# GroupNorm over 134 MB: weights of the identity loaded once a tile, and loops without a remainder

## The chip, the cores and the metric

The kernel runs on one core of one Trainium2 chip. The metric is the device time of one execution in microseconds (us), given as the median of several runs. A profiled execution gives a trace beside it: for each engine, what ran when, and for the DMA engines their packets and landings. Times inside the trace count from the start of its span.

## The reference

The input x has 128 images of 1024 channels of 32 x 16 values in bf16. The channels form 32 groups of 32. Each group of each image is normalised by its own mean and variance, and each channel then gets a scale and an offset:

```python
xr = x.reshape(B, G, C // G, H, W)
mu = xr.mean(axis=(2, 3, 4), keepdims=True)
var = ((xr - mu) ** 2).mean(axis=(2, 3, 4), keepdims=True)
xn = (xr - mu) / jnp.sqrt(var + 1e-5)
xn = xn.reshape(B, C, H, W)
return xn * g[None, :, None, None] + b[None, :, None, None]
```

So 134 MB are read and 134 MB are written, and each value is needed twice: for the statistics and for the result.

## The kernel before

One tile is four images: 128 partitions (4 images x 32 groups), each with the 16,384 values of one group, 32 KB a partition and 4 MB in all. There are NT = 32 tiles and SLOTS = 6 buffers x0 to x5 in SBUF; tile i uses buffer i % 6. Every buffer has its own small tiles (nshift, sq, negmean and so on) and its own semaphores.

All loads and stores are issued by SyncE (SP), in an order written out by hand: the six first loads, with the two small ones for g and b behind the first; then for each tile i its store, followed by the load of tile i + 5. A store waits until VectorE is done with the tile (s_done); a load waits until the store that empties its buffer has landed (s_store). At the end SyncE waits for the last store of every buffer.

Three engines work on a tile, each in its own loop:

- TensorE (`sums`, L181): 32 matmuls of an identity matrix (`eye`) with 512 columns of the tile each, accumulated in one PSUM bank ps. This adds up the 32 parts of each partition. Every matmul call issues two instructions: LDWEIGHTS, which loads the identity into the array, and MATMUL.
- ScalarE (`squares`, L194): the mean of the first 512 values as a shift (L197), then four passes over a quarter of the tile each that sum the squares of the shifted values (L208); after VectorE's variance the square root (L217).
- VectorE (`normalise`, L221): the sum of ps gives the mean (L224); with ScalarE's squares the variance (L235 to L248), the reciprocal of the root, scale and offset per channel (L258 to L264); then 32 instructions that write the result over the tile in place, one for each channel of the group (L274).

The loops are real loops on the engines, with a counter in a register. One iteration holds the code of six tiles, one for each buffer; the counter gives the values that the semaphores are waited for. As 32 is not a multiple of 6, there are ROUNDS = 5 iterations, and behind them the code of REST = 2 more tiles:

```python
with act.Fori(1, ROUNDS + 1) as n:
    n16 = act.snap(n * 16)
    for j in range(SLOTS):
        squares(j, n16, n)
for j in range(REST):
    squares(j, 16 * (ROUNDS + 1), ROUNDS + 1)
```

[...]

Of the kernel before, what the change touches and what calls it, by code (L numbers as in the profile page):

```python
# [16 lines left out]
SLOTS = 6  # L17
MM_FREE = 512
# [4 lines left out]
def kernel(  # L23
# [13 lines left out]
    nc = tc.nc  # L37
# [6 lines left out]
    NT = B0 // NS  # L44
    F = KC * HW
    inv_n = 1.0 / float(F)
    NMM = F // MM_FREE
    SQ = F // SQ_PARTS

    x_v = x.rearrange("(t n) (q k) h w -> t (n q) (k h w)", n=NS, q=G)  # L50
    o_v = out.rearrange("(t n) (q k) h w -> t (n q) (k h w)", n=NS, q=G)
# [5 lines left out]
    def sb(name, shape, dtype):  # L57
        return ctx.enter_context(nc.sbuf_tensor(name, shape, dtype))

    def sem(name):  # L60
        return tc.alloc_semaphore(name)

    xs = [sb(f"x{j}", [P, F], BF16) for j in range(SLOTS)]
    ps = [
        ctx.enter_context(nc.psum_tensor(f"ps{j}", [P, MM_FREE], F32))
        for j in range(SLOTS)
    ]
# [9 lines left out]
    eye = sb("eye", [P, P], BF16)  # L77
    ja = sb("ja", [P, HW], BF16)
    js = sb("js", [P, SQ], BF16)
    jd = sb("jd", [P, MM_FREE], BF16)  # L80
# [16 lines left out]
    def sems(name):  # L97
        return [sem(f"{name}{j}") for j in range(SLOTS)]

    s_load = sems("load")  # L100
    s_store = sems("store")
# [19 lines left out]
    sp, pe, act, dve, pool = nc.sync, nc.tensor, nc.scalar, nc.vector, nc.gpsimd  # L121

    def load(i):
        j, n = i % SLOTS, i // SLOTS
        if n > 0:
            sp.wait_ge(s_store[j], 16 * n)
        sp.dma_start(out=xs[j][:], in_=x_v[i]).then_inc(s_load[j], 16)  # L127

    def store(i):
        j, n = i % SLOTS, i // SLOTS  # L130
        sp.wait_ge(s_done[j], n + 1)
        sp.dma_start(out=o_v[i], in_=xs[j][:]).then_inc(s_store[j], 16)

# [2 lines left out]


    load(0)
    sp.dma_start(out=gam_b[:], in_=four(g_v)).then_inc(s_gb, 16)
    sp.dma_start(out=bet_b[:], in_=four(b_v)).then_inc(s_gb, 16)  # L140
    for i in range(1, SLOTS):
        load(i)
    for i in range(NT):
        store(i)
        if i >= 1 and i + SLOTS - 1 < NT:
            load(i + SLOTS - 1)
    for j in range(SLOTS):
        sp.wait_ge(s_store[j], 16 * len(range(j, NT, SLOTS)))


    dve.memset(eps_t[:], EPS).then_inc(s_eps, 1)  # L151
# [3 lines left out]
        out=half[:],  # L155
# [9 lines left out]
        out=eye[:],  # L165
# [12 lines left out]
    dve.wait_ge(s_gbf, 1)  # L178
    pe.wait_ge(s_eye, 1)

    def sums(j, n16):  # L181

        pe.wait_ge(s_load[j], n16)
        for k in range(NMM):
            m = pe.matmul(  # L185
                out=ps[j][:],
                lhsT=eye[:],
                rhs=xs[j][:, k * MM_FREE : (k + 1) * MM_FREE],
                start=(k == 0),
                stop=(k == NMM - 1),  # L190
            )
        m.then_inc(s_sum[j], 1)

    def squares(j, n16, n):  # L194

        act.wait_ge(s_load[j], n16)
        act.activation(  # L197
            out=ja[:],
            in_=xs[j][:, 0:HW],
            func=ACT.Identity,  # L200
            scale=-1.0 / HW,
            accum_out=nshift[j][:],
        ).then_inc(s_shift[j], 1)
        act.wait_ge(s_shift[j], n)
        for k in range(SQ_PARTS):
            if k > 0:
                act.wait_ge(s_part[k - 1][j], n)
            act.activation(  # L208
                out=js[:],
                in_=xs[j][:, k * SQ : (k + 1) * SQ],  # L210
                func=ACT.Square,
                bias=nshift[j][:],
                scale=1.0,
                accum_out=sq[j][:, k : k + 1],
            ).then_inc(s_part[k][j], 1)
        act.wait_ge(s_var[j], n)
        act.activation(  # L217
            out=std[j][:], in_=var[j][:], func=ACT.Sqrt, bias=eps_t[:], scale=1.0
        ).then_inc(s_std[j], 1)

    def normalise(j, n):  # L221

        dve.wait_ge(s_sum[j], n)
        dve.tensor_scalar(  # L224
            out=jd[:],
            in0=ps[j][:],
            scalar1=-inv_n,
            scalar2=None,
            op0=ALU.mult,
            op1=ALU.add,  # L230
            accum_out=negmean[j][:],
        ).then_inc(s_mean[j], 1)
        dve.wait_ge(s_mean[j], n)
        dve.wait_ge(s_part[SQ_PARTS - 1][j], n)  # L234
        dve.tensor_tensor(  # L235
            out=d[j][:], in0=negmean[j][:], in1=nshift[j][:], op=ALU.subtract
        ).then_inc(s_d[j], 1)
        dve.wait_ge(s_d[j], n)
        dve.tensor_scalar(  # L239
            out=nd2[j][:],  # L240
            in0=d[j][:],
            scalar1=d[j][:],
            scalar2=-1.0,
            op0=ALU.mult,
            op1=ALU.mult,
        ).then_inc(s_nd2[j], 1)
        dve.wait_ge(s_nd2[j], n)
        dve.tensor_scalar(  # L248
            out=jv[:],
            in0=sq[j][:],  # L250
            scalar1=inv_n,
            scalar2=nd2[j][:],
            op0=ALU.mult,
            op1=ALU.add,
            accum_out=var[j][:],
        ).then_inc(s_var[j], 1)
        dve.wait_ge(s_std[j], n)
        dve.reciprocal(out=rstd[j][:], in_=std[j][:]).then_inc(s_rstd[j], 1)  # L258
        dve.wait_ge(s_rstd[j], n)
        dve.tensor_scalar(  # L260
            out=scl[j][:], in0=gam[:], scalar1=rstd[j][:], scalar2=None, op0=ALU.mult
        ).then_inc(s_scl[j], 1)
        dve.wait_ge(s_scl[j], n)
        dve.scalar_tensor_tensor(  # L264
            out=bia[j][:],
            in0=scl[j][:],
            scalar=negmean[j][:],
            in1=bet[:],
            op0=ALU.mult,
            op1=ALU.add,  # L270
        ).then_inc(s_bia[j], 1)
        dve.wait_ge(s_bia[j], n)
        for k in range(KC):
            v = dve.tensor_scalar(  # L274
                out=xs[j][:, k * HW : (k + 1) * HW],
                in0=xs[j][:, k * HW : (k + 1) * HW],
                scalar1=scl[j][:, k : k + 1],
                scalar2=bia[j][:, k : k + 1],
                op0=ALU.mult,
                op1=ALU.add,  # L280
            )
        v.then_inc(s_done[j], 1)


    ROUNDS = NT // SLOTS
    REST = NT % SLOTS
    with pe.Fori(16, 16 * ROUNDS + 1, 16) as n16:
        for j in range(SLOTS):
            sums(j, n16)
    for j in range(REST):  # L290
        sums(j, 16 * (ROUNDS + 1))

    with act.Fori(1, ROUNDS + 1) as n:
        n16 = act.snap(n * 16)
        for j in range(SLOTS):
            squares(j, n16, n)
    for j in range(REST):
        squares(j, 16 * (ROUNDS + 1), ROUNDS + 1)

    with dve.Fori(1, ROUNDS + 1) as n:  # L300
        for j in range(SLOTS):
            normalise(j, n)
    for j in range(REST):
        normalise(j, ROUNDS + 1)


# [28 lines left out]
```

## Time and profile before

| | |
|---|---|
| median of 3 runs | 634.16 us (633.76 to 634.39) |
| the profiled execution | 634.32 us |
| its span | 632.6 us, so 1.72 us lie outside |
| bytes moved | 268.53 MB, mean 424 GB/s |
| ScalarE, VectorE busy | 519.3 us (82%), 395.0 us (62%) |
| TensorE: matmuls, weight loads | 286.1 us (45%), 112.7 us (18%) |
| one tile on ScalarE (four passes of L208) | 4 x 3,708 ns |
| weight load, median | 98 ns, 1,024 of them |
| load and store, median from issue to landing | 29.2 us, 38.4 us |

The profile's page gives busy times by engine, the span in 40 slices, the DMA queues and the chain of work that ended last. In the views of stretches each row has the stretch, its length, the busy time of PE (matmuls), PEld (weight loads), VectorE, ScalarE and GpSimd with the number of instructions, the TensorE clock granted, the busy share of the 16 DMA engines, and GB/s. A row of the chain has start, duration and what ran. In the waits a row has who waited for whom, the sum in us, how many times, and the longest.

### The profile page before, as it was taken

How to read it: one execution, taken by the hardware profiler on the slowest of the kernel's cores; microseconds unless marked ns; L12 is line 12 of the kernel's file. 1: busy time of each engine (PE TensorE's matmuls, PEld its weight loads, DVE VectorE, ACT ScalarE, POOL GpSimd, SP SyncE). 2: the span in 40 equal slices, each digit the busy share in tenths (PEclk: the TensorE clock that was granted, in tenths of full speed). 3: DMA queues.
4: the chain of work that ended last, by engine and by line, in shares of the span. 5: the costliest groups of instructions: out<-in, count | busy, mean ns of one | idle time of the engine just before them, and what ended most of it. 6: DMA issues, size and time to landing. Idle time of an engine off the chain costs nothing.

```text
span 632.6 us, 3913 instructions
## 1 busy us (share of the span) xinstructions
PE 286.1 (45%) x1007; PEld 112.7 (18%) x1024; DVE 395.0 (62%) x1316; ACT 519.3 (82%) x354; POOL 0.8 (0%) x6
## 2 busy tenths in 40 slices
PE   1977404553245632456433655334553335643300
PEld 0332101221112211122111222111221112221100
DVE  0177777766666667777655676555775556765550
ACT  2999999999999999997878978789888889887700
POOL 0000000000000000000000000000000000000000
PEclk9988858766787667876678776678765787666755
DMA  9999999999999999999999999999999999999994
GB/s 366 431 430 417 434 433 431 433 429 427 435 431 429 433 431 433 437 433 433 435 431 433 429 431 431 431 435 433 431 433 433 437 431 437 433 430 431 433 431 204
DMA packets 9487, 268.53 MB, mean 424 GB/s; under 512 B 1288, under 2 KB 1288, under 8 KB 1288
## 3 DMA queue, kind: packets, MB, share of 16 engines
q1 hardware_dynamic: 9480, 268.46, 98.7%
q8 instruction: 2, 0.03, 0.0%
q14 instruction: 5, 0.04, 0.0%
HBM read 134.23 MB, written 134.22 MB: 424 GB/s over the span
## 4 chain that ended last, share of the span: by engine, by line
DMA 73%; ACT 18%; DVE 4%; SPq 1%; issue 0%; DVEq 0%
DMA out_dram<-x 67%; ACT js L208 17%; DMA x<-in_x_dram 7%; DVE x L274 3%; ACT ja L197 1%; SPq L127 1%; ACT std L217 0%; DVE jv L248 0%; DVE nd L239 0%; DVE d L235 0%; DVE bia L264 0%; DVE scl L260 0%; DVE rstd L258 0%; DVEq L234 0%; DVEq L300 0%
## 5 line engine op out<-in xcount | busy, mean ns | idle before, releaser
L208 ACT ACTIVATE js<-x,nshift 128x4096 bf16<-128x4096 bf16 x128 | 474.7, 3708 | 4.1
L185 PE MATMUL ps<-x,eye 128*128 128x512 bf16 x1007 | 286.1, 451 | 304.3 <-DMA x<-in_x_dram 302.5
L274 DVE TENSOR_SCALAR x<-x,scl,bia 128x512 bf16<-128x512 bf16 x1024 | 333.7, 422 | 1.2
L185 PEld LDWEIGHTS ps<-x,eye 128*128 128x128 bf16 x1024 | 112.7, 113 | 477.2 <-DMA x<-in_x_dram 317.8
L235 DVE TENSOR_TENSOR d<-negmean,nshift 128x1 f32<-128x1 f32 x32 | 5.1, 160 | 167.3 <-ACT js L208 167.3
L197 ACT ACTIVATE ja<-x 128x512 bf16<-128x512 bf16 x32 | 19.9, 623 | 47.9 <-DMA x<-in_x_dram 47.7
L224 DVE TENSOR_SCALAR_CACHE_REDUCE jd<-ps 128x512 bf16<-128x512 f32 x32 | 22.5, 703 | 16.4 <-PE ps L185 16.2
L217 ACT ACTIVATE std<-var,eps_t 128x1 f32<-128x1 f32 x32 | 9.4, 294 | 25.8 <-DVE jv L248 25.8
L208 ACT ACTIVATION_READ_ACCUMULATOR js<-x,nshift 128x1 f32 x128 | 23.9, 186 | 0.0
L258 DVE RECIPROCAL rstd<-std 128x1 f32<-128x1 f32 x32 | 5.2, 164 | 11.6 <-ACT std L217 11.6
L264 DVE SCALAR_TENSOR_TENSOR bia<-scl,negmean,bet 128x32 f32<-128x32 f32 x32 | 8.1, 252 | 1.1
L260 DVE TENSOR_SCALAR scl<-gam,rstd 128x32 f32<-128x32 f32 x32 | 7.7, 242 | 1.1
L176 DVE CAST gam<-gam_b 128x32 f32<-128x32 bf16 x1 | 0.2, 181 | 12.4 <-DMA bet_b<-in_b_dram 12.4
L248 DVE TENSOR_SCALAR_CACHE_REDUCE jv<-sq,nd 128x4 f32<-128x4 f32 x32 | 7.0, 218 | 1.1
L239 DVE TENSOR_SCALAR nd<-d 128x1 f32<-128x1 f32 x32 | 6.8, 214 | 1.1
L197 ACT ACTIVATION_READ_ACCUMULATOR ja<-x 128x1 f32 x32 | 6.0, 186 | 0.0
L224 DVE DVE_READ_ACCUMULATOR jd<-ps 128x1 f32 x32 | 3.2, 99 | 0.0
L248 DVE DVE_READ_ACCUMULATOR jv<-sq,nd 128x1 f32 x32 | 2.7, 84 | 0.0
L174 ACT ACT_TABLE_LOAD x1 | 1.3, 1283 | 1.0 <-SPq L55 1.0
L151 DVE MEMSET eps_t<- 128x1 f32 x1 | 0.1, 59 | 1.1 <-SPq L55 1.1
L154 POOL TENSOR_SCALAR_AFFINE_SELECT half<-ones 128x128 bf16<-128x128 bf16 x1 | 0.3, 292 | 0.9 <-DVE ones L152 0.9
L164 POOL TENSOR_SCALAR_AFFINE_SELECT eye<-half 128x128 bf16<-128x128 bf16 x1 | 0.3, 292 | 0.1
(7 smaller groups left out, 0.9 us busy)
## 6 DMA issues: line engine op xcount, KB each, us to landing
x<-in_x_dram SPq DMA_DIRECT2D x32, 4096.0 KB, 29.2
out_dram<-x SPq DMA_DIRECT2D x32, 4096.0 KB, 38.4
gam_b<-in_g_dram SPq DMA_DIRECT2D x1, 8.0 KB
bet_b<-in_b_dram SPq DMA_DIRECT2D x1, 8.0 KB
```

The costliest lines, as they stand in the source:

```text
L127: sp.dma_start(out=xs[j][:], in_=x_v[i]).then_inc(s_load[j], 16)
L185: m = pe.matmul(out=ps[j][:], lhsT=eye[:], rhs=xs[j][:, k * MM_FREE : (k + 1) * MM_FREE], start=(k == 0), stop=(k == NMM - 1),)
L197: act.activation(out=ja[:], in_=xs[j][:, 0:HW], func=ACT.Identity, scale=-1.0 / HW, accum_out=nshift[j][:],).then_inc(s_shift[j], 1)
L208: act.activation(out=js[:], in_=xs[j][:, k * SQ : (k + 1) * SQ], func=ACT.Square, bias=nshift[j][:], scale=1.0, accum_out=sq[j][:, k : k + 1],
L217: act.activation(out=std[j][:], in_=var[j][:], func=ACT.Sqrt, bias=eps_t[:], scale=1.0).then_inc(s_std[j], 1)
L224: dve.tensor_scalar(out=jd[:], in0=ps[j][:], scalar1=-inv_n, scalar2=None, op0=ALU.mult, op1=ALU.add, accum_out=negmean[j][:],).then_inc(s ...
L239: dve.tensor_scalar(out=nd2[j][:], in0=d[j][:], scalar1=d[j][:], scalar2=-1.0, op0=ALU.mult, op1=ALU.mult,).then_inc(s_nd2[j], 1)
L248: dve.tensor_scalar(out=jv[:], in0=sq[j][:], scalar1=inv_n, scalar2=nd2[j][:], op0=ALU.mult, op1=ALU.add, accum_out=var[j][:],).then_inc(s ...
L258: dve.reciprocal(out=rstd[j][:], in_=std[j][:]).then_inc(s_rstd[j], 1)
L260: dve.tensor_scalar(out=scl[j][:], in0=gam[:], scalar1=rstd[j][:], scalar2=None, op0=ALU.mult).then_inc(s_scl[j], 1)
L264: dve.scalar_tensor_tensor(out=bia[j][:], in0=scl[j][:], scalar=negmean[j][:], in1=bet[:], op0=ALU.mult, op1=ALU.add,).then_inc(s_bia[j], 1)
L274: v = dve.tensor_scalar(out=xs[j][:, k * HW : (k + 1) * HW], in0=xs[j][:, k * HW : (k + 1) * HW], scalar1=scl[j][:, k : k + 1], scalar2=bi ...
```

## The change

In `sums` only the first matmul of a tile loads the identity. The other 31 are written as bare MATMUL instructions that use the weights already in the array (`again`).

The loops have six iterations and no code behind them. Six iterations of six buffers would be 36 tiles, so in the first iteration the four buffers 0 to 3 are skipped by a branch (`If`). Tile i therefore uses buffer (i + 4) % 6: tiles 0 and 1 use buffers 4 and 5, tile 2 buffer 0, and so on. In the later iterations buffers 0 to 3 wait for counts that are lower by one than those of buffers 4 and 5, hence the second set of registers (m, m16).

```diff
+    FIRST = -NT % SLOTS
+    ROUNDS = (NT + FIRST) // SLOTS
...
     def load(i):
-        j, n = i % SLOTS, i // SLOTS
+        j, n = (i + FIRST) % SLOTS, i // SLOTS
...
     def store(i):
-        j, n = i % SLOTS, i // SLOTS
+        j, n = (i + FIRST) % SLOTS, i // SLOTS
...
     for j in range(SLOTS):
-        sp.wait_ge(s_store[j], 16 * len(range(j, NT, SLOTS)))
+        sp.wait_ge(s_store[j], 16 * len(range((j - FIRST) % SLOTS, NT, SLOTS)))
...
+    def again(first, rhs, stop):
+
+        return pe.add_instruction(
+            mybir.InstMatmult(
+                name=nc.get_next_instruction_name(),
+                ins=[pe.lower_ap(rhs), first.ins[1]],
+                outs=[first.outs[0]],
+                start_tensor_calc=False,
+                stop_tensor_calc=stop,
+                tile_size=first.tile_size,
+                tile_position=first.tile_position,
+                ldweights=False,
+            )
+        )
+
     def sums(j, n16):
 
         pe.wait_ge(s_load[j], n16)
-        for k in range(NMM):
-            m = pe.matmul(
-                out=ps[j][:],
-                lhsT=eye[:],
-                rhs=xs[j][:, k * MM_FREE : (k + 1) * MM_FREE],
-                start=(k == 0),
-                stop=(k == NMM - 1),
-            )
+        m = pe.matmul(out=ps[j][:], lhsT=eye[:], rhs=xs[j][:, 0:MM_FREE], start=True, stop=False)
+        for k in range(1, NMM):
+            m = again(m.ins, xs[j][:, k * MM_FREE : (k + 1) * MM_FREE], k == NMM - 1)
         m.then_inc(s_sum[j], 1)
...
-    ROUNDS = NT // SLOTS
-    REST = NT % SLOTS
...
     with act.Fori(1, ROUNDS + 1) as n:
         n16 = act.snap(n * 16)
-        for j in range(SLOTS):
+        m, m16 = act.snap(n - 1), act.snap(n16 - 16)
+        with act.If(n > 1):
+            for j in range(FIRST):
+                squares(j, m16, m)
+        for j in range(FIRST, SLOTS):
             squares(j, n16, n)
-    for j in range(REST):
-        squares(j, 16 * (ROUNDS + 1), ROUNDS + 1)
```

The loops of TensorE and VectorE are changed in the same way.

More of the change, by code (lines that the diff above doesn't have):

```diff
@@ L282, in normalise @@
         v.then_inc(s_done[j], 1)
-    ROUNDS = NT // SLOTS
-    REST = NT % SLOTS
     with pe.Fori(16, 16 * ROUNDS + 1, 16) as n16:
-        for j in range(SLOTS):
+        m16 = pe.snap(n16 - 16)
+        with pe.If(n16 > 16):
+            for j in range(FIRST):
+                sums(j, m16)
+        for j in range(FIRST, SLOTS):
             sums(j, n16)
-    for j in range(REST):
-        sums(j, 16 * (ROUNDS + 1))
     with act.Fori(1, ROUNDS + 1) as n:
         n16 = act.snap(n * 16)
-        for j in range(SLOTS):
+        m, m16 = act.snap(n - 1), act.snap(n16 - 16)
+        with act.If(n > 1):
+            for j in range(FIRST):
+                squares(j, m16, m)
+        for j in range(FIRST, SLOTS):
             squares(j, n16, n)
-    for j in range(REST):
-        squares(j, 16 * (ROUNDS + 1), ROUNDS + 1)
     with dve.Fori(1, ROUNDS + 1) as n:
-        for j in range(SLOTS):
+        m = dve.snap(n - 1)
+        with dve.If(n > 1):
+            for j in range(FIRST):
+                normalise(j, m)
+        for j in range(FIRST, SLOTS):
             normalise(j, n)
-    for j in range(REST):
-        normalise(j, ROUNDS + 1)
 _INS = ['x', 'g', 'b']
```

## The prediction

> **What bounds the kernel now.** I read the page's totals first, then the DMA queues, then the chain of work that ended last, then what SyncE's queue waited for, and last the stretches after the final load.
>
> ```profile
> PE 286.1 (45%) x1007; PEld 112.7 (18%) x1024; DVE 395.0 (62%) x1316; ACT 519.3 (82%) x354; POOL 0.8 (0%) x6
> ...
> DMA  9999999999999999999999999999999999999994
> ...
> q1 hardware_dynamic: 9480, 268.46, 98.7%
> q8 instruction: 2, 0.03, 0.0%
> q14 instruction: 5, 0.04, 0.0%
> ```
>
> No compute engine is full; the 16 DMA engines are, in every slice but the last. The two "instruction" queues are loads of the engines' own code, by the same DMA engines. They are seven packets, but they matter below.
>
> ```profile
> 551.84 29.14 DMA x<-in_x_dram
> ...
> 581.00 0.73 ACT ja L197 x2
> ...
> 598.96 10.43 DVE x L274 x32
> ```
>
> From the end of the chain of waits: the last load lands at 580.98, ScalarE and VectorE work on that tile until 609.4, and then its store goes out. It lands at 630.0. So is this chain of 28.4 us of compute the end of the kernel? The stretches say no:
>
> ```profile
> 581.00:609.00 28.00, 9.32 (x31) 3.62 (x32) 20.94 (x69) 16.22 (x11) 0.00 (x0) 0.62 1.00 433
> ...
> 612.00:615.00 3.00, 0.00 (x0) 0.00 (x0) 0.00 (x0) 0.00 (x0) 0.00 (x0) 0.50 1.01 437
> ...
> 621.00:624.00 3.00, 0.00 (x0) 0.00 (x0) 0.00 (x0) 0.00 (x0) 0.00 (x0) 0.50 0.76 328
> 624.00:627.00 3.00, 0.00 (x0) 0.00 (x0) 0.00 (x0) 0.00 (x0) 0.00 (x0) 0.50 0.23 98
> 627.00:629.60 2.60, 0.00 (x0) 0.00 (x0) 0.00 (x0) 0.00 (x0) 0.00 (x0) 0.50 0.12 50
> ```
>
> The last two columns are the DMA engines' busy share and GB/s. DMA is full while the last tile is computed. The last store waits behind its predecessors, and then the engines finish unevenly: 0.23 of 16 is four engines still at work, 0.12 is two.
>
> The trace's landing records say the same of each engine. Every transfer is marked 16 times, once by each DMA engine. Of the last store's marks, eleven lie between 623.4 and 624.2; the others are at 625.2, 627.6, 628.8, 629.7 and 630.0. The sum of the profiled execution is therefore:
> - the first data packet starts at 2.0;
> - an engine moves 512 packets of 32 KB (64 transfers of 4 MB over 16 engines); the median packet takes 1.213 us, so 621.1, which gives 623.1;
> - the last engine lags the first mark (623.4) by 6.65, which gives 630.0;
> - 2.6 of closing steps gives the span of 632.6, and 1.7 outside it gives 634.32. The median of the runs is 634.16, so 0.16 lower.
>
> Only the number of bytes, the rate and the lag enter. The bytes don't change.
>
> **The change, part by part.**
>
> *Weights once a tile.* 31 of 32 LDWEIGHTS go, 98 ns each by the median: 3.0 us of PE per tile. With the clock up, tile 0 takes 9.9 us on PE (13.43 to 23.33), so I put it at 6.9 afterwards; the ends are 9.9 (the load was hidden) and 6.9. All of it is beside the path, as two rows of the waits show:
>
> ```profile
> DVE d L235 <- ACT js L208: 167.3, 32, 6.7
> ...
> DVE jd L224 <- PE ps L185: 16.2, 10, 9.4
> ```
>
> VectorE waits for PE ten times, but for ScalarE's squares after that in every one of the 32 tiles. A faster PE lengthens the second wait. Value: 0, on both sides. If the cover were gone (ScalarE done before PE), it would be worth up to 3.0 us in the last tile alone, and even that lies before the backlog described next.
>
> *The new tile order of the loops.* The instructions done per tile are the same. Added per iteration and engine: a subtraction or two, a compare-and-branch, the end of the branch's body. The trace has such steps: around the loop's end VectorE's ALU step takes 0.05, its branch 0.07, its move 0.05; PE's branch takes 0.21. I take 0.2 us, between 0.1 and 0.4, six times per engine: about 1.2 us. ScalarE hides it in the 47.7 us that it waits for loads, PE in 302.5. After the last load only one tile follows (tile 31), with no new branch in front of it but what was already passed at tile 26.
>
> And if something in the last tile's chain did come later? The last store is issued at 609.4. The earlier ones keep the first engine to be free busy until about 623.4 - 9.7 = 613.7 (a store is 8 packets of 1.213 on each engine), and the last engine until about 620.3. So 4.3 us of delay cost nothing on any engine, and up to 10.9 nothing at the end. Nor would a gain there show.
>
> *The first iteration's jump.* PE and ScalarE reach their loops at 2.1 and 1.2 us, and the first load lands at 13.4: 11 us of cover. VectorE reaches its loop at 14.2 and waits for PE until 23.3: 9 us of cover. The first six stores are issued 12 to 22 us before the DMA engines come to them (issue against the first mark of the transfer ahead), so a late tile 0 or 1 starves nothing. Is a taken branch dear? The one that the trace has is not:
>
> ```profile
> 123.30 0.07 DVEq L300
> 123.37 0.03 issue
> 123.39 0.28 DVE x L274
> ```
>
> There is no gap in it for a load of code. [...]
>
> *Buffers renumbered, final waits.* Tile 0 goes to buffer 4; the order of the DMAs on SyncE's queue and what each waits for are the same. The closing waits keep their number; the last store's buffer is now the sixth instead of the second. Worth 0, within 0.1.
>
> *Less code, other code loads.* This is the one part that touches the DMA engines. Within the span the trace has a load of 16 KB at 39.2 (1.06 us) and at 566.5 (0.96), and loads of 8 KB at 50.6, 77.9, 102.6, 602.3 (0.31 to 0.33 each) and 631.7, in the closing steps. Each takes an engine out of step. After 39.2, one engine marks its next landing 0.9 behind the 15th; after 102.6 the latest goes from 2.4 to 3.2 us behind the first; after 566.5 a punctual engine falls back by 1.2; and around 602.3 the last engine goes from 6.32 to 6.69. Engines that are behind then lose more, 0.3 to 0.5 us in a packet where loads and stores alternate: the lags grow to 3 to 5 us by 300 and stay at 4.2, 5.4 and 5.9 from about 450 on.
>
> The times fit where VectorE stands after every further 128 instructions (8 KB) and PE after every 256 (16 KB); 77.9 fits ScalarE. In the new program PE's loop has 6 x 33 instructions in place of 6 x 64, and no engine has two tiles behind the loop. So 566.5 (PE in those tiles) and 602.3 (VectorE in its 32nd tile) go, 39.2 goes or moves to PE's first iteration, 77.9 moves ahead of the first load, and VectorE's two early ones move to about 14 and 35. What is that worth? 602.3 hit the engine that ended last: 6.69 - 6.32 = 0.4. 566.5 hit one that didn't: 0. For the early ones the ends are far apart. If an engine put out of step at 35 grows to the same lag as those of 39 and 51 did, 0. If the lag stops at 4.24, as of the engine that began to fall back near 150 with no code load beside it, 6.65 - 4.24 = 2.4. If no engine lags (the eleven punctual ones spread by 0.85), 5.8. I take 0, because the nearest row is the load at 39.2, which was early too and still grew.
>
> [...]
>
> Sum: 634.16 - 0.4 = 633.7.
>
> **The rivals.**
> 1. *The lag really shrinks (faster).* With fewer and earlier disturbances the last engine stays at 4.2 (631.8) or lower, to 628.4 without lag. For it: the steps at 39.2, 102.6 and 602.3. Against: one engine reached 4.24 without such a step, and it takes only one.
> 2. *A late code load hits the engine that is last (slower).* The new code may have a boundary that PE or VectorE crosses in the last 60 us, at the loop's end. A 16 KB load there costs what it cost at 566.5: 0.96 and 0.47 more in the packet beside it, 1.4 in all, so 635.6. It decides only if it falls on the engine that ends last; the loads of 8 KB (0.3 to 0.65) would not leave the band.
> 3. *Nothing changes at all*: the same lag comes about whatever the code; 634.2. Also if LDWEIGHTS were still issued.
>
> **How the numbers follow.** About 0.2% (1.3 us) is what a measurement of this kernel can tell from no change. My forecast, a few tenths less (633.7), gets 0.36, rival 3 gets 0.14: both "same", 0.50. Rival 1 gets 0.36, and of it some 0.22 lies above 631.2. Rival 2, and a lag that grows in another way, get 0.14, half of it under 635.6. The range 631.2 to 635.6 holds 0.50 + 0.22 + 0.08 = 0.80; the likeliest case alone has 633.0 to 634.5.
>
> **What would show it.** Right: PEld falls to 32 instructions and PE's busy time by a quarter or more; DVE's wait for PE shrinks while that for ScalarE grows; the steady stretches stay at 431 to 434 GB/s; the last load lands near 581 again; code loads between 540 and 610 are gone and the last store's marks still spread over 5 to 6.5 us. Wrong: fewer than two engines at work after 625 (rival 1), a code load of 16 KB after 540 (rival 2), or a dip of the DMA share before 609, which would mean a stall in the loops that I cost at nothing.

## The result, and the profile after

The changed kernel takes 633.21 us (median of 14 runs, 632.48 to 635.28), the kernel before 634.16 (14 runs, 633.76 to 635.2). The ratio is 0.9985, 95% interval 0.9978 to 0.9991: 0.95 us less, between 0.6 and 1.4. Run again later beside other kernels it gave 0.9987 (0.9978 to 0.9996). That is a real gain, below the 0.2% that the forecast called a difference; the forecast was 633.7.

The profiled execution took 633.21 us, its span 631.5. From the page of the changed kernel, the rows that answer to those of before:

```profile
PE 284.3 (45%) x1024; PEld 3.3 (1%) x32; DVE 394.8 (63%) x1316; ACT 519.3 (82%) x354; POOL 0.8 (0%) x6
...
DMA  8999999999999999999999999999999999999995
...
q1 hardware_dynamic: 9480, 268.46, 98.9%
q14 instruction: 4, 0.03, 0.0%
q8 instruction: 1, 0.02, 0.0%
```

The 992 weight loads are gone from PEld (112.7 to 3.3 us), and the matmuls took about as long as before (286.1 us, with 17 of 1,024 records missing from the trace, and 284.3 us). A quick tile shows it best; the first row is from the kernel before, where the tile has 32 weight loads (one of its 32 matmuls is not recorded), the other two from the changed kernel, where it has one:

```profile
43.68 7.08 PE L185 MATMUL ps<-x,eye 128*128 128x512 bf16 x31 [2.03 <-DMA x<-in_x_dram]
...
24.53 0.39 PE L202 MATMUL ps<-x,eye 128*128 128x512 bf16 x1 [1.04 <-DMA x<-in_x_dram]
24.75 6.85 PE L186 MATMUL ps<-x,eye 128*128 128x512 bf16 x31
```

That is 7.08 us before, and 7.07 us after (24.53 to 31.60). VectorE, ScalarE and the bytes are the same. There are two loads of code fewer. The waits of the changed kernel:

```profile
DVE d L248 <- ACT js L221: 169.2, 32, 6.7
...
DVE jd L237 <- PE ps L186: 13.1, 8, 8.8
```

VectorE waits 3.1 us less for PE and 1.9 us more for ScalarE, still in each of the 32 tiles. The end of the chain:

```profile
551.46 29.02 DMA x<-in_x_dram
...
580.51 0.73 ACT ja L210 x2
...
605.25 3.63 DVE x L287 x11
```

The last load lands at 580.49 (580.98 before) and the last store goes out at about 608.9 (609.4 before). And the stretches after it, with the DMA engines' busy share and GB/s in the last two columns:

```profile
621.00:624.00 3.00, 0.00 (x0) 0.00 (x0) 0.00 (x0) 0.00 (x0) 0.00 (x0) 0.50 0.81 350
624.00:627.00 3.00, 0.00 (x0) 0.00 (x0) 0.00 (x0) 0.00 (x0) 0.00 (x0) 0.50 0.25 109
627.00:629.60 2.60, 0.00 (x0) 0.00 (x0) 0.00 (x0) 0.00 (x0) 0.00 (x0) 0.50 0.03 13
```

Between 627.0 and 629.6 the share was 0.12 before and is 0.03 now. That is where the time went. The marks of the last store say it in full: the first at 623.54 (623.37 before), the last 5.36 us later (6.65 before), at 628.90 (630.02). With the closing steps and what lies outside the span, 4.31 in this execution and 4.30 in that of before, this gives the two times. The same identity held in every profiled execution of the study: time = first mark of the last store + lag of the last engine + 4.3 us (4.29 to 4.36). The first mark moved by at most 0.6 us among the kernels with their last store on time (623.35 to 623.91). So what is left to explain is mainly the lag, which ran from 5.36 to 7.86 us in the same executions.

### The profile page after: what moved, and what is told of

It is laid out like the page before. It is cut to its first block, busy times and chain, and to the rows that moved or that the text cites. A ratio compares the mean times of both kernels' runs of the same rounds, so it can differ in the third digit from the quotient of the medians.

```text
span 631.5 us, 2991 instructions
## 1 busy us (share of the span) xinstructions
PE 284.3 (45%) x1024; PEld 3.3 (1%) x32; DVE 394.8 (63%) x1316; ACT 519.3 (82%) x354; POOL 0.8 (0%) x6
## 4 chain that ended last, share of the span: by engine, by line
DMA 73%; ACT 18%; DVE 4%; issue 1%; SPq 1%; DVEq 0%; ACTq 0%
DMA out_dram<-x 66%; ACT js L221 17%; DMA x<-in_x_dram 7%; DVE x L287 3%; ACT ja L210 1%; SPq L130 1%; ACT std L230 0%; DVE jv L261 0%; DVE nd L252 0%; DVE d L248 0%; DVE bia L277 0%; DVE scl L273 0%; DVE rstd L271 0%; DVEq L247 0%; ACTq L307 0%
## 5 line engine op out<-in xcount | busy, mean ns | idle before, releaser
L186 PE MATMUL ps<-x,eye 128*128 128x512 bf16 x992 | 272.4, 443 | 0.0
L202 PE MATMUL ps<-x,eye 128*128 128x512 bf16 x32 | 18.4, 574 | 305.7 <-DMA x<-in_x_dram 305.7
L202 PEld LDWEIGHTS ps<-x,eye 128*128 128x128 bf16 x32 | 3.3, 103 | 577.3 <-DMA x<-in_x_dram 577.3
```

The lines of the kernel that those rows point to most:

```text
L186: return pe.add_instruction(mybir.InstMatmult(name=nc.get_next_instruction_name(), ins=[pe.lower_ap(rhs), first.ins[1]], outs=[first.outs[0]],
L202: m = pe.matmul(out=ps[j][:], lhsT=eye[:], rhs=xs[j][:, 0:MM_FREE], start=True, stop=False)
```

## The experiments

Theory A, from the prediction: loads of code put DMA engines behind, they stay behind, and the last one sets the end. Rival B: the weight loads themselves did it. Rival C: the lag belongs to the loads and stores, code or no code. Rival D: the compute of the last tile sets the end. All ratios are to the kernel before, on the same chip.

**Each half alone.** First the weights once a tile in the old loops (only `sums` changed, as in the diff of the change):

> Half of the change alone: 31 of 32 weight loads of a tile are gone, the loops are those of before (five iterations and two tiles behind them). Theory A (the kernel ends with the DMA engine that lags most, and loads of code put engines behind): VectorE's code is as long as before, so its loads of 8 KB come near 51, 103 and 602 us again; the last store's marks spread over 6.0 to 6.7 us, and the time is that of before within 0.3 us, 633.9 to 634.4. Rival B (the gain comes from the weight loads that PE no longer issues): the time of the changed kernel, 633.2, and a spread of about 5.4 us.

Measured: 1.0001 (0.9993 to 1.0010). Taking out the weight loads alone gives nothing. VectorE's code loads came at 50.7, 102.2 and 601.9 us as before, and the last engine went from 6.68 us behind to 7.47 around the last of them; at the end it was 7.43, more than the 6.0 to 6.7 expected.

Then the new loops alone, with a weight load before every matmul as in the old `sums`:

> The other half alone: six iterations with the skip in the first, every matmul loads the identity again. Theory A: VectorE's late load near 602 us is gone and its early ones move before 40 us; the spread of the last store's marks is 5.0 to 5.8 us and the time 633.0 to 633.6. PE's code is 416 instructions instead of 230, so there may be one load of 16 KB more. Rival B: 634.2 as before.

Measured: 0.9999 (0.9990 to 1.0007). The late load was gone, as expected, and its trace has a lag of 6.39 nevertheless (5.0 to 5.8 expected). So neither half has the gain alone. PE's longer code brought a load of 16 KB at 6.6 us.

**The remainder in front, no branch.**

```diff
+    for j in range(FIRST, SLOTS):
+        normalise(j, 1)
+    with dve.Fori(1, ROUNDS) as n:
+        m = dve.snap(n + 1)
+        for j in range(FIRST):
+            normalise(j, n)
+        for j in range(FIRST, SLOTS):
+            normalise(j, m)
```

> The changed kernel without the branch: the two extra tiles stand in front of a loop of five iterations, so VectorE's code is as long as before (366 instructions for 8 tiles) and has as many 8 KB loads, but all of them are in the first 130 us. If the late load near 602 us is what the change saved: spread 5.0 to 5.8 us, 633.0 to 633.6. If the number of loads counts, wherever they are: spread 6.0 to 6.7, 634.0 to 634.4. If shorter code counts through the loads that come when loads and stores already alternate (after 70 us), it is between: one or two of them come there, 633.4 to 634.2.

Measured: 0.9987 (0.9978 to 0.9996), 0.88 us less in the medians. The gain needs neither the branch nor short VectorE code; this kernel has five loads of code between 51 and 155 us, and its lag was 5.55. What it shares with the changed kernel are weights once a tile, tiles that begin at buffer 4, and, in these two traces, no load of code between 155 and 630 us (a second trace of the changed kernel, below, has one at 236.0). The new order of the buffers was not tried by itself; the run with the loops alone has it too, and no gain.

**Late loads of code.**

```diff
         for j in range(FIRST, SLOTS):
             normalise(j, n)
+    for _ in range(400):
+        dve.wait_ge(s_gbf, 1)
```

> The changed kernel with 201 idle instructions (waits that are already met) on VectorE behind its loop, so that its code crosses two more boundaries of 128 instructions after 609 us, when all its work is done but DMA is still busy. In the changed kernel the 8 KB load at 34.9 us fell on the engine that ended last. Theory A: if VectorE's loads still go to that engine, each costs 0.3 to 0.65 us at the end: spread 6.0 to 6.7 us, time 633.8 to 634.5. Rival C (lags are set by the transfers alone, code loads are only beside them): 633.2, spread 5.4.

Measured: 1.0013 (1.0004 to 1.0022), against 0.9985 and 0.9987 of the changed kernel without them: some 1.7 us dearer. In its trace the loads came at 613.3 and 626.1; the last engine's lag was 4.63 us on the transfer that began to land at 604.5, 5.12 on the next and 5.89 on the last. So this costs, and more than the 0.3 to 0.65 us that were expected of each load: the lag grew by 0.5 and 0.8 around the two, and the medians say 1.7 in all. (The traced execution, 634.05 us, was the fastest of the eleven.) The idle instructions run from 608 us on; that they cost nothing by themselves is assumed, as no run has them at that place without the loads.

**No computing, no code.** In place of `sums`, `squares` and `normalise`:

```diff
+    def light(j, n16):
+        dve.wait_ge(s_load[j], n16)
+        dve.tensor_scalar(out=xs[j][:, 0:HW], in0=xs[j][:, 0:HW],
+            scalar1=gam[:, 0:1], scalar2=bet[:, 0:1],
+            op0=ALU.mult, op1=ALU.add).then_inc(s_done[j], 1)
```

> The changed kernel with nearly all computing left out: no PE and no ScalarE work, and VectorE does one instruction per tile on its first channel, so the output is not the normalised one. The loads and stores and their order on the queue stay. The loops are so short (VectorE 35 instructions in all) that no code is loaded within the span. Theory A: the lag of the last engine is smaller, what the engines drift apart without a push: 3.3 to 4.8 us, and the time 631 to 632.7. Rival C (lags belong to the transfers alone): 5.4 to 6.7 us and 633.2 to 634.4.

Measured: 0.9997 (0.9987 to 1.0007). From its page, and its stretches (without PE's two columns):

```profile
span 632.6 us, 206 instructions
...
q14 instruction: 1, 0.01, 0.0%
```

```profile
624.00:627.00 3.00, 0.00 (x0) 0.00 (x0) 0.00 (x0) 1.00 0.25 109
627.00:629.60 2.60, 0.00 (x0) 0.00 (x0) 0.00 (x0) 1.00 0.09 38
```

The one load of code is in the closing steps. 206 instructions in place of 3,913, no statistics, almost no writing by VectorE: the same time, and engines that end as unevenly. The last was 1.46 us behind at 62, 4.81 at 246, 6.21 at 362 and 6.62 at the end. Here the first half of theory A falls. The lag does not need code loads; with loads and stores alone it builds up, and levels off. Rival C is right on that. It also speaks against the number of code loads as what the change gained by: this kernel, which leaves out the computing as well, has none before the closing steps and no gain that can be told; the changed kernel has four and a gain.

**The same with code loads early.**

```diff
+    for _ in range(1200):
+        dve.wait_ge(s_gbf, 1)
     with dve.Fori(1, ROUNDS + 1) as n:
```

> The same, with 600 idle instructions (waits that are already met) on VectorE ahead of its loop, after the first load: four to five loads of 8 KB of code between 15 and 45 us, no other change. Theory A: one engine is put back by 0.3 to 1 us by each and stays the last: lag 1 to 2.5 us more than without them, the time too. Rival C: the same time as without them, within 0.3 us.

Measured: 1.0256 (1.0239 to 1.0273), 16.5 us more, and for another reason than expected. An idle instruction took 0.10 us (600 of them from 14.4 to 74.6 us), more than I had counted, so VectorE reached its first tile only at 75 us. From the page:

```profile
DMA  9997399999999999999999999999999999999994
GB/s 365 435 425 330 130 420 412 428 422 450 420 436 436 424 442 424 436 432 424 436 428 436 432 424 438 426 436 434 428 436 426 436 436 428 440 424 432 436 432 209
```

In the fourth and fifth slice (49 to 81 us) the DMA engines ran out of work. As a test of early loads it is spoilt. It shows something else: while the code was loading, one engine fell 4.79 us behind (at 61 us; without the loads it was 1.46 at 62); the pause wiped that out (0.58 at 97 us); and then, without another load of code before the closing steps, the lag grew again, to 3.34 at 321 and 6.17 at the end.

**Is the last tile's compute covered?** Extra VectorE instructions in the last tile alone:

```diff
+        for i in range(extra):
+            dve.tensor_scalar(
+                out=jd[:], in0=ps[j][:], scalar1=1.0, scalar2=None, op0=ALU.mult
+            ).then_inc(s_slow, 1)
+            dve.wait_ge(s_slow, i + 1)
         for k in range(KC):
```

> The kernel before, with five more VectorE instructions of about 0.7 us in the last tile alone, one after another, ahead of its 32 result instructions: the last store is issued some 3.7 us later, at about 613. Theory A (backlog of the DMA engines: 4.3 us for the first engine, 10.9 for the last): no change, within 0.3 us of the kernel before. Rival D (the compute of the last tile sets the end): 3.7 us more, 637.9.

> The same with 22 such instructions: the last store is issued some 16 us later. Theory A: the last engine's backlog of 10.9 us is used up, so 5 to 6 us more than before, 639 to 640.5. Rival D: 16 us more, 650.

Measured with 5: 1.0002 (0.9993 to 1.0012). With 22: 1.0106 (1.0089 to 1.0122), 641.02 us, 6.8 more. The trace of the latter has 15.92 us in the 22 instructions, and then:

```profile
609.00:624.00 15.00, 0.00 (x0) 0.00 (x0) 14.69 (x36) 0.00 (x0) 0.00 (x0) 0.50 0.37 159
```

The DMA engines run dry, as they don't in the kernel before, where the same stretch is:

```profile
609.00:624.00 15.00, 0.00 (x0) 0.00 (x0) 0.38 (x2) 0.00 (x0) 0.00 (x0) 0.50 0.96 413
```

Expected were 5 to 6 us; by the traces, 637.0 against 630.0 for the last mark is 7.0. The backlog is real, and its size right within 1 to 2 us: 16 us of delay cost 6.8, 3.6 cost nothing. Rival D is out.

**Is it the weights or the length of PE's code?** The changed kernel with idle instructions on PE:

```diff
         m.then_inc(s_sum[j], 1)
+        for _ in range(62):
+            pe.wait_ge(s_eye, 1)
```

> The changed kernel with 31 idle instructions (waits that are already met) behind each tile's matmuls on PE: the weights are loaded once a tile, but PE's code is as long as in the run with the loops alone (417 instructions against 416). If that run lost the gain by its longer PE code and the 16 KB that it loads at 6.6 us: a 16 KB load before 10 us here too, last engine's lag 6 or more, and the time of the kernel before, ratio 0.9995 to 1.0005. If it lost the gain by the 1,024 weight loads themselves: the time of the changed kernel, ratio 0.998 to 0.999.

Measured: 1.0005 (0.9996 to 1.0014), beside 0.9987 (0.9978 to 0.9996) of the changed kernel in the same comparison. The gain is gone with no weight load added. The 16 KB load was there, at 6.4 us, and the lag was 7.11. Together with the halves (1.0001 with weights alone; 0.9999 and 1.0005 with long PE code, with and without the weight loads) rival B is out as the whole cause: taking the weight loads out gave nothing in two kernels. What PE runs besides does matter. Whether it is the load at 6.4 us or the idle instructions themselves, this run can't tell, but its trace speaks against the early load: the lag was 4.35 us at 236 and 5.13 at 420 (4.57 and 5.33 in the changed kernel), and grew to 7.13 only from there to 604 us, a time in which no code was loaded.

**Only the late load moved.** First in the kernel before, then together with the weights once a tile:

```diff
+    for _ in range(160):
+        dve.wait_ge(s_eps, 1)
     dve.wait_ge(s_gb, 32)
```

> The kernel before, all weight loads and its loops as they were, with 80 idle instructions (waits that are already met) at the head of VectorE's code, where it waits for 12 us anyway. They shift the boundaries of 128 instructions, so that the one that was crossed in the last tile (the load near 602 us) is crossed in the loop's first iteration, near 125 us. If that late load on the last engine was the cost: ratio 0.9985 to 0.9993, lag 5.4 to 6.0. If the gain has to do with the weights, with the branch or with the number of loads: ratio 1.000.

> The kernel before with both: weights once a tile and the 80 idle instructions on VectorE that move the late load, but still five iterations and two tiles behind them. If the late load is all: ratio 0.9985 to 0.9993, as with the 80 instructions alone. If late load and weight loads each keep the lag up, so that both have to go: 0.998 to 0.999 here, and 1.000 with the instructions alone. If it takes the new loops: 1.000 in both.

Measured: 0.9996 (0.9986 to 1.0005) and 0.9994 (0.9985 to 1.0003). Both hold 1.000 and the expected gain. The loads moved as intended: VectorE's to 11.5, 69.1 and 120.6 us in the first, none near 602 in either. But the lags were 6.17 (5.4 to 6.0 expected) and 7.86, the largest of all. The times decide nothing; the traces show that a large lag needs no late load of VectorE's code.

**The changed kernel again**, in the same comparison:

> The changed kernel itself again, beside these on the same chip: 0.9978 to 0.9991 as measured first; the last store's marks spread over 5.0 to 5.8 us with no load of code between 540 and 625 us.

Measured: 0.9987 (0.9978 to 0.9996). But its profiled execution took 634.43 us and had a lag of 6.62, outside the 5.0 to 5.8 expected, where the first one took 633.21 and had 5.36; PE's 16 KB load came at 236.0 us instead of 117.3. So the lag of one execution differs from the next by as much as the whole effect. The times of many runs carry the verdicts; a single trace shows the mechanism but not the mean.

## Why the prediction was right, and where it wasn't

*What bounds the kernel* was right: transfers, and the lag of the last DMA engine. The run without computing has the same time, and the identity of first mark, lag and 4.3 us holds in all of them.

*Weights once a tile, cost 0*: right in the sum, shown by the run with the weights alone. The step behind it was wrong. I took a weight load as standing between two matmuls and put tile 0 at 6.9 us instead of 9.9. Tile 0 took 9.5 us afterwards (13.96 to 23.48), and the run with the weights alone has 286.9 us of matmuls, against 286.1 before. The weight loads were hidden behind the matmuls already, and the trace before had a row that says so, the tile with 32 of them in 7.08 us. Tile 0 is longer for another reason: in both kernels its matmuls start 0.43 us apart until about 19 us, and 0.22 apart from then on. So "PE's busy time by a quarter or more" did not come, and VectorE's wait for PE shrank by 3.1 us only.

*Loops, jump, buffers, cost 0*: right. DMA stays at 430 to 435 GB/s through the steady stretches, the form without the branch does as well, and the backlog that covers the last tile was tested from both sides. VectorE took the jump at 15.1 us and its next load of code came at 19.4; PE's sum, which it needed next, was there only at 23.5 (its longest wait for PE, 8.8 us).

*Less code, 0.4 us*: the sign was right, the size too small. The measured gain is 0.95 (0.6 to 1.4). That the forecast came this near is in part luck: the 0.4 is what one load near 602 us did to the lag in one execution. In the three other traces that have this load the step was 0.80 (weights alone), 0.13 and 0.04 (5 and 22 delays). Of the loads, those at 566.5 and 602.3 went and VectorE's early ones came at 19.4 and 34.9 (about 14 and 35 expected). Wrong: 77.9, ScalarE's, went to 6.5, after the first packets and not before them; and PE's of 39.2 moved to 117.3, not to the first iteration. That a load on the last engine late in the kernel can cost 0.4 us or more is made likely by the run with two more of them.

The step that failed is the one that tied the *growing* of the lag to the loads of code. An engine falls 6.6 us behind with no code loaded at all, as rival 3 said of the lag. Its other half, that the time would stay, is refuted. Rival 1 came in part: the first trace shows a smaller lag, 5.36, but the second 6.62, so it is a shift of a mean by about 1 us, not a lag that vanishes. Rival 2 did not come; the run with late loads shows that it could have, at 1.7 us for two loads of 8 KB.

*Open*: what the 0.95 us consist of. By the packet records the load near 602 us puts one engine back by 0.65 (0.30 for its own packet, and the next data packet takes 1.56 us instead of 1.21), and this counts only as far as that engine ends last. That fits the small steps in the lag; the one of 0.80 is more than it accounts for. Moving it alone was not resolved (0.9996, 0.9986 to 1.0005). Why more instructions on PE cost the gain is not settled. The two runs with PE's 16 KB load at 6.4 to 6.6 us had no gain, those with it at 69.3, 117.3 and 236.0 had one, and the one with it at 432.0 was not resolved; that is a coincidence of places until a run moves that load alone. A lag set at the start does not carry through in these traces: 2.12 us at the first load went with 6.39 at the end (loops alone), 0.62 with 6.62 (no computing).

*How many engines lag*: three to seven ended over 1 us behind the first in these traces, five in the kernel before and five in the changed one. Where no code is loaded in the span ahead of it, the marks of the first load lie 0.56 us (the kernel before) and 0.62 us (no computing) apart, and a pause of the queue set the engines level again (0.17 us apart at 87 us, after 4.79 at 61).

## What to carry to other kernels

Where the DMA engines are full from start to end, computing can cost nothing: here nearly all of it could be left out without a change (0.9997). What is left is the last engine's lag, and it is read from the sixteen landing marks of the last store, not from busy shares. Look where code is loaded: near the end a load can fall on the engine that ends last (steps of 0.04 to 0.80 us here), and in the changed kernel, whose code ends inside its loop, none came between 236 and 630 us. For effects of 0.1 to 0.2% compare many runs of one chip; one trace of each kernel would here have shown 1.3 us between two executions of the same program.

## What the runs showed of the hardware that was not expected

- The engines drift apart without computing or code loads: 6.62 us between the first and the last after 64 transfers of 4 MB, in the run without computing. In the traces whose queue stayed full to the end it was 5.36 to 7.86 us.
- The levelling off is not final: in the runs with 22 delays, with idle instructions on PE, and with 80 of them on VectorE the lag stood at 5.07, 5.25 and 4.33 us near 450 to 460, and at 6.18, 6.53 and 5.55 near 556, with no code loaded in between. The cause is not known.
- A queue that ran empty set them level: 4.79 us at 61 us, 0.17 at 87 and 0.58 at 97 us after a pause; and 0.17 for the last store of the run with 22 delays, against 6.65 before.
- Weight loads of 128 columns between matmuls of 512 columns cost PE no time that can be seen: a tile took 7.08 us with 32 of them and 7.07 with one, at 98 ns each by their own rows.
- A wait that is already met, as an instruction of its own, takes VectorE 0.10 us (600 of them from 14.4 to 74.6 us).
- In the same program PE's code load of 16 KB came at 117.3 us in one execution and at 236.0 in another.
